# Float32 attention items whose product with v is turned and divided at the end, and three weight pieces asked for later

## The chip, the core and the metric

The kernel runs on one core of one Trainium2 chip. The metric is device microseconds for one execution, the median of three runs. A core has engines with queues of their own that run side by side: TensorE (PE) for matmuls, which writes to PSUM; VectorE (DVE) and ScalarE (ACT) for elementwise work, which read PSUM and SBUF; GpSimd (POOL), which reads SBUF alone; and SyncE (SP), whose queue issues the DMAs here. Each queue is strictly in order; engines wait for one another by semaphores.

## The reference

Windowed causal attention (4 batches, 8 heads, 576 positions, head size 64, window 128, with a bias that falls with distance), and after it two feed-forward layers over 2304 tokens, 512 to 2048 to 512. The weights are float64.

```python
scores = scale * np.matmul(q, k.transpose(0, 1, 3, 2))
scores = np.where(mask, scores + bias[None], -1000000000.0)
attn = np.exp(scores - np.max(scores, axis=-1, keepdims=True))
attn = attn / (np.sum(attn, axis=-1, keepdims=True) + 1e-09)
x = np.matmul(attn, v)            # then [tokens, 512]
h = x @ w_in
g = np.maximum(h, 0.0) + alpha * np.minimum(h, 0.0)
x = g @ w_out
# second layer: g = h * sigmoid(1.702 h), again two products
```

## The kernel before

Attention is cut into 64 items: a batch, a head, and the first 256 or the last 320 of the positions. The first 16 items (n < FP), the first 256 positions of two batches, are done in plain float32; each of their matmuls shows as two passes in the trace. All later products are done with each operand split into a high and a low part (names ending in h and l) and three matmuls, high by high, high by low and low by high.

A float32 item goes through these steps. QK (L343): scores of two chunks of 128 queries, against 128 and 256 keys, with K=64. Bias (L363, DVE): bias and mask are added and the row's least value is taken (the scores have their sign turned). Exp (L379, ACT), with the sum of each row read out by the same instruction. Reciprocal (L387 and L388, DVE) of the sum plus 1e-9. Normalization: the first chunk on DVE (L399), the second on ACT (L397). Three transpositions of 128x128 on PE (L412) and one copy out of PSUM on ACT (L419, pt). Then the product with v (L433): v stands still, pt moves, so the result x has head dimensions on partitions and queries on columns. v was copied by POOL (L329) into a tile of 128 columns that is zero but for the 64 of its head, even or odd; so the two heads of a pair add up in one PSUM tile of 128x256. After the odd head x is split (L480 on ACT, xh; L107 on DVE, xl): that is one of four blocks (c) of 128 rows of the first layer's input.

The weights come as float64, 32 pieces of 512 KB for the first layer. A piece goes: load (L131, SP), two scalings of its words on ACT (L147, L148), then on DVE sign (L152), shift (L157), add (L162), which frees its load buffer (four of them), and a split into a high part (L102 on ACT, L103 on DVE for two of them) and a low part wl (L107, DVE).

The program is written as a loop of 10 steps ahead of the first token block; each step issues parts of several items and the steps of two weight pieces. Then come token blocks of 256 with 16 steps each (f); a step is a feed-forward product h (L494, 12 matmuls, two PSUM buffers), the activation (n, L509 on ACT; g, L519 on DVE; split gh, gl) and, two steps later, the second product o (L545, 12 matmuls); one attention item is spread over two steps. The first block also takes a weight piece per step. A scheduler that runs its own timeline while it builds the program sets the order on each engine, so the order of the queues is not that of the code. The program's first feed-forward products, f=0 and 1, run in four parts, as the blocks c of x come. The later blocks, the second layer and its output are the same in both kernels.

Of the kernel before, what the change touches and what calls it, by code (L numbers as in the profile page):

```python
# [11 lines left out]
F32 = mybir.dt.float32  # L12
# [3 lines left out]
AF = mybir.ActivationFunctionType  # L16
ALU = mybir.AluOpType
PSUM = bass.MemoryType.PSUM

B, H, S, D = 4, 8, 576, 64  # L20
NT, DM, DFF = 2304, 512, 2048
P = 128
# [12 lines left out]
         chunks=((256, 128, 128, 256), (384, 128, 256, 256), (512, 64, 384, 192))),  # L35
# [12 lines left out]
FP = 2 * H  # L48
# [17 lines left out]
def tile_window_attention__then__two_mlps(  # L66
# [13 lines left out]
    nc = tc.nc  # L80
# [10 lines left out]
    ident = const.tile([P, P], F32, name="ident")  # L91
# [129 lines left out]
    def w(step, lim=2 * NF):  # L221

        names = ("load", "scale", "sign", "shift", "add", "split")
        i = wdone.get(step, 0)
        if i < min(lim, wdone.get(names[names.index(step) - 1], 0)):
            {"scale": w_scale, "sign": w_sign, "shift": w_shift, "add": w_add, "split": w_split}[step](i)
            wdone[step] = i + 1

    def w_ahead():
        if wdone.get("add", 0) >= 2 * NF and ("x", 0) not in p2:  # L230
            return
        i = wdone.get("load", 0)
        while i < min(wdone.get("add", 0) + NST, len(chunks)):
            w_load(i)
            i += 1
        wdone["load"] = i

    def w_decode(lim):
        w("sign", lim)
        w("shift", lim)  # L240
        w("add", lim)
        w_ahead()
        w("scale", lim)
# [21 lines left out]

    af = ExitStack()
    apf = af.enter_context(tc.tile_pool(name="attf", bufs=1))
    vzs = [apf.tile([P, 2, P], F32, name=f"vz{i}") for i in range(2)]
    pts = [apf.tile([P, 384], F32, name=f"pt{i}") for i in range(2)]
    relht = apf.tile([P, H, 2 * P], BF16, name="relht")  # L270

# [13 lines left out]
    st = {}  # L285
# [37 lines left out]
    @stage  # L323
    def a_split_v(n, b, u, h, U):
        nv = (2, 4)[u]
        vr = raw_of(n)[:, UCOLS[u] - nv * D : UCOLS[u]].rearrange("p (j d) -> p j d", d=D)
        if n < FP:
            d0 = (h % 2) * D
            nc.gpsimd.tensor_copy(vzs[n % 2][:, :, d0 : d0 + D], vr)  # L329
            return  # L330
        vp = ar["v", n % 2]
        nc.scalar.copy(vp[:, :nv, :D], vr)
        sub("pool", vp[:, :nv, D:], vr, vp[:, :nv, :D])
# [40 lines left out]
    @stage  # L374
    def a_exp(n, b, u, h, U):
        tt, s = tts[n % 2], sts[n % 2]
        for i, (c0, rows, kk, keys) in enumerate(U["chunks"]):
            t = tt[:rows, i * 256 : i * 256 + keys]
            nc.scalar.activation(  # L379
                t, t, AF.Exp, bias=s[:rows, i : i + 1], scale=-1.0, accum_out=s[:rows, 4 + i : 5 + i]  # L380
            )

    @stage
    def a_recip(n, b, u, h, U):
        s = sts[n % 2]
        m = len(U["chunks"])
        nc.vector.tensor_scalar(s[:, 8 : 8 + m], s[:, 4 : 4 + m], 1e-9, None, op0=ALU.add)  # L387
        nc.vector.reciprocal(s[:, 12 : 12 + m], s[:, 8 : 8 + m])  # L388

    @stage  # L390
    def a_norm(n, b, u, h, U, eng):
        tt, s = tts[n % 2], sts[n % 2]
        for i, (c0, rows, kk, keys) in enumerate(U["chunks"]):
            t = tt[:rows, i * 256 : i * 256 + keys]
            r = s[:rows, 12 + i : 13 + i]
            if eng == "act" or (eng == "mix" and i):
                nc.scalar.mul(t, t, r)  # L397
            else:
                nc.vector.tensor_scalar(t, t, r, None, op0=ALU.mult)  # L399
# [27 lines left out]
    @stage  # L427
    def a_av(n, b, u, h, U):
        if n < FP:
            x = st["x", n] = st["x", n - 1] if h % 2 else ps_a.tile([P, 512], F32, tag="a", name="x")  # L430
            pt, vz = pts[n % 2], vzs[n % 2]
            for j in range(2):
                nc.tensor.matmul(  # L433
                    x[:, j * P : 256], vz[:, j, :], pt[:, j * 256 : 256 + j * P],
                    start=(h % 2 == 0 and j == 0), stop=(h % 2 == 1 and j == 1), skip_group_check=True,
                )
            return
        vp = ar["v", n % 2]
        x = ps_a.tile([P, 512], F32, tag="a", name="x")
        js = (0, 1) if u == 0 else (2, 1, 3, 4)  # L440
        for i, j in enumerate(js):
            col, nq, oc = PTCOL[u][j]
            v = vp[:, j - U["k0"] // P, :]
            for k, p in enumerate((ar["pth"], ar["ptl"])):
                nc.tensor.matmul(  # L445
                    x[:, oc : oc + nq], v, p[:, col : col + nq],
                    start=(i == 0 and k == 0), stop=(i == len(js) - 1 and k == 1),
                    skip_group_check=True,
                )
        st["x", n] = x  # L450
# [17 lines left out]
    @stage  # L468
    def a_x3(n, b, u, h, U):
        if h % 2 == 0:  # L470
            return
        nq, c, xp = U["nq"], h // 2, xps
        if n < FP:
            xp = st["x", n]
        t = u * B * UNITS[0]["nq"] + b * nq
        done = 0
        while done < nq:
            r = (t + done) % RING
            w = min(nq - done, RING - r)
            nc.scalar.copy(xh[:, c, r : r + w], xp[:, done : done + w])  # L480
            sub("dve", xl[:, c, r : r + w], xp[:, done : done + w], xh[:, c, r : r + w])
            done += w
# [222 lines left out]


    for t in vzs:
        nc.gpsimd.memset(t, 0.0)
    for t in sts:
        nc.gpsimd.memset(t, 1.0)  # L710
    def w_first(n):
# [22 lines left out]
    for n in range(H + 2):  # L734

        a_av(n - 2)
        a_split_v(n)
        if n + 4 < H + 2:
            a_load(n + 4)
        if n >= H:  # L740
            a_load(n + 2)
        if n + 1 < H + 2:
            a_qk(n + 1)
        a_bias(n)
        w("split")
        w("sign")
        a_exp(n)
        a_recip(n - 1)
        w("shift")
        a_norm(n - 1, "mix")  # L750
        a_trans(n - 1)
        w("add")
        w_ahead()
        w("scale")
        a_x3(n - 2)
        w("split")
        w("sign")
        w("shift")
        a_pt_hi(n - 1, 0)
        a_pt_hi(n - 1, 1)  # L760
        if n + 2 < H + 2:
            a_split(n + 2)
        w("add")
        w_ahead()
        w("scale")
    n = H + 2
    a_split(n)
    for i in range(2):
# [12 lines left out]
    for s, (k, f) in enumerate(steps):  # L781
        n = H + 2 + s // 2
        norm = "mix" if k == 0 else "dve"
        if (k, f) == (KM, 0):
            pinned.append(True)
        dec = k == 0 or k == KM
        lim = min(3 * NF, max(W1, wdone["split"]) + 3) if k else W1

        def wd(*names):
            for x in names if dec else ():  # L790
                w(x, lim)

        m = n - 1
        m1_h(k, f)
        if s % 2 == 0:
            a_trans(m)
            a_qk(n)
            a_pt_hi(m, 0)
            m1_n(k, f)
            wd("sign")  # L800
            m1_g(k, f)
            a_pt_hi(m, 1)
            a_bias(n)
            wd("shift")
            a_pt_lo(m, 0)
            a_pt_lo(m, 1)
            wd("add", "scale")
            w_ahead()
            a_split(n + 1)
            a_exp(n)  # L810
            m1_lo(k, f, "dve")
        else:
            a_av(m)
            if n == FP:
                a_parts()
            a_recip(n)
            a_split_v(n)
            a_load(n + 2)
            a_norm(n, norm)
            m1_n(k, f)  # L820
            wd("sign")
            m1_g(k, f)
            a_x1(n - 1)
            wd("shift", "scale")
            a_x2(n - 1)
            wd("add")
            w_ahead()
            m1_lo(k, f, "dve")
            a_x3(n - 1)
        if k == 0:  # L830
            w("split")
        m1_o(k - (f < LAG), (f - LAG) % NF)
        if n == NI + 1 and s % 2:
            at.close()
            p2["ps"] = ctx.enter_context(tc.tile_pool(name="ps_p", bufs=1, space=PSUM))
            p2["x", 0] = ctx.enter_context(tc.tile_pool(name="p20", bufs=1))
            pre = ExitStack()
            p2["g1"] = pre.enter_context(tc.tile_pool(name="g1", bufs=3))
            p2["n1"] = pre.enter_context(tc.tile_pool(name="n1", bufs=2))
            w_ahead()  # L840
        if k == KM:
            w("split", min(3 * NF, W1 + 2 * (f - 2)))
            if f >= 8 and f % 2 == 0:
                x2_split(0, f // 2 - 4)
            if f >= 6 and f % 2 == 0 and f < 14:
                x2_load(0, f // 2 - 3)
# [117 lines left out]
```

## Time and profile before

| what | value |
|---|---|
| median of 3 runs | 968.03 us (967.75 to 969.53) |
| the profiled execution | 967.92 us, span 966.1 us |
| PE busy | 939.6 us, 97% of the span |
| DVE busy | 721.6 us, 75% |
| ACT busy | 536.4 us, 56% |
| POOL busy | 89.8 us, 9% |
| chain that ended last | PE 92%, DMA 3%, ACT 2%, DVE 1% |

The span is the time from the first to the last instruction; the run's own time is 1.8 us longer. PE is busy nearly all the time, but matmuls overlap and their ends are modelled, so the start of one and the start of the next tell more than the busy share. The rows below are from the first 140 us, where the changed code runs. Names of tiles stand without buffer numbers; L and a number are a line of the kernel.

### The profile page before, as it was taken

To read this page: it belongs to the slowest core of one execution; us is meant where nothing else is said; L and a number is where in the kernel's file an instruction comes from. 1 tells how busy PE (TensorE), PEld (TensorE's weight loads), DVE (VectorE), ACT (ScalarE), POOL (GpSimd) and SP (SyncE) were. 2 spreads that over 40 slices of the span, in tenths; PEclk is the share of its full clock that TensorE was granted. 3 is DMA by queue.
4 is the path that set the end of the run, shared out by engine and by line. 5 is a ranking of instruction groups with operands and counts; after the bars stand their busy time and mean duration, and the time that the engine had idled before them with its cause. 6 is when DMAs were issued, how large, how long until landed. Compare 5 with 4: busy or idle time off the path is not lost.

```text
span 966.1 us, 17886 instructions
## 1 busy us (share of the span) xinstructions
PE 939.6 (97%) x6536; PEld 871.2 (90%) x6536; DVE 721.6 (75%) x1789; ACT 536.4 (56%) x1343; POOL 89.8 (9%) x127
## 2 busy tenths in 40 slices
PE   5899999999999999999999999999999999999997
PEld 3579889999999999999988888888898889999997
DVE  6998967767888888887666864697233798878876
ACT  6987766666767667676534443564232644333433
POOL 1000021122222222222000000000000000000000
PEclk9999999999999999999999999999999999999999
DMA  8654521222222223212022335566432333443323
GB/s 266 187 185 148 184 79 56 78 72 66 89 67 88 67 66 89 67 66 89 1 69 81 124 112 182 186 219 200 155 113 88 140 140 114 142 142 113 132 85 109
DMA packets 43895, 112.44 MB, mean 116 GB/s; under 512 B 5024, under 2 KB 15008, under 8 KB 43808
## 3 DMA queue, kind: packets, MB, share of 16 engines
q1 hardware_dynamic: 43808, 111.31, 35.3%
q8 instruction: 51, 0.84, 0.3%
q14 instruction: 36, 0.29, 0.1%
HBM read 82.98 MB, written 28.31 MB: 115 GB/s over the span
## 4 chain that ended last, share of the span: by engine, by line
PE 92%; DMA 3%; ACT 2%; DVE 1%; issue 1%; SPq 0%; DVEq 0%; ACTq 0%
PE h L494 21%; PE h L592 20%; PE p L659 17%; PE o L545 17%; PE p L545 5%; PE x L445 3%; PE pt L412 3%; DMA ws<-in_w_out_dram 2%; PE s L352 1%; PE s L353 1%; PE s L343 1%; PE x L433 1%; ACT ws L148 1%; DMA ws<-in_w_in_dram 0%; ACT oh L102 0%
## 5 line engine op out<-in xcount | busy, mean ns | idle before, releaser
L494 PE MATMUL h<-xh,wh 128*128 128x256 f32 (+1 forms) x512 | 153.7, 302 | 1.0 <-ACT xh L480 0.7
L494 PE MATMUL h<-xh,wl 128*128 128x256 f32 (+1 forms) x512 | 153.6, 300 | 0.0
L494 PE MATMUL h<-xl,wh 128*128 128x256 f32 (+1 forms) x512 | 153.5, 300 | 0.1
L659 PE MATMUL p<-wh,oh 128*128 128x256 f32 x504 | 136.2, 284 | 1.0 <-ACT oh L102 0.6
L659 PE MATMUL p<-wl,oh 128*128 128x256 f32 x504 | 136.1, 283 | 0.0
L545 PE MATMUL o<-gh,wl 128*128 128x256 f32 x448 | 127.5, 286 | 0.0
L545 PE MATMUL o<-gh,wh 128*128 128x256 f32 x448 | 125.4, 286 | 0.0
L545 PE MATMUL o<-gl,wh 128*128 128x256 f32 x448 | 125.2, 281 | 0.0
L659 PE MATMUL p<-wh,ol 128*128 128x256 f32 x504 | 119.2, 284 | 1.0 <-DVE ol L107 1.0
L592 PE MATMUL h<-x2h,wh 128*128 128x512 f32 (+1 forms) x320 | 117.8, 368 | 0.0
L592 PE MATMUL h<-x2l,wh 128*128 128x512 f32 (+1 forms) x320 | 117.7, 368 | 0.0
L592 PE MATMUL h<-x2h,wl 128*128 128x512 f32 (+1 forms) x320 | 117.7, 368 | 0.0
L606 DVE TENSOR_TENSOR g<-h,sg 128x512 f32<-128x512 f32 (+1 forms) x80 | 51.0, 637 | 79.6 <-ACT sg L602 79.5
L602 ACT ACTIVATE sg<-h 128x512 f32<-128x512 f32 (+1 forms) x80 | 44.5, 556 | 107.2 <-PE h L592 106.9
L494 PEld LDWEIGHTS h<-xh,wh 128*128 128x128 f32 x512 | 97.9, 192 | 6.7 <-ACT xh L480 1.9
L494 PEld LDWEIGHTS h<-xl,wh 128*128 128x128 f32 x512 | 98.5, 192 | 5.0 <-DVE st L388 1.3
L494 PEld LDWEIGHTS h<-xh,wl 128*128 128x128 f32 x512 | 98.3, 192 | 2.9
L659 PEld LDWEIGHTS p<-wh,oh 128*128 128x128 f32 x504 | 96.4, 192 | 2.1 <-ACT oh L102 2.0
L659 PEld LDWEIGHTS p<-wl,oh 128*128 128x128 f32 x504 | 96.7, 192 | 0.1
L519 DVE SCALAR_TENSOR_TENSOR g<-n,beta,h 128x256 f32<-128x256 f32 x112 | 53.2, 476 | 46.6 <-ACT n L509 46.4
L659 PEld LDWEIGHTS p<-wh,ol 128*128 128x128 f32 x504 | 86.3, 192 | 1.7 <-DVE ol L107 1.6
L509 ACT ACTIVATE n<-h 128x256 f32<-128x256 f32 x112 | 42.8, 384 | 79.9 <-PE h L494 79.5
(107 smaller groups left out, 2270.7 us busy)
## 6 DMA issues: line engine op xcount, KB each, us to landing
ws<-in_w_in_dram SPq DMA_DIRECT2D x32, 512.0 KB, 3.6
ws<-in_w_out_dram SPq DMA_DIRECT2D x32, 512.0 KB, 3.9
raw<-in_u_dram SPq DMA_DIRECT2D x32, 512.0 KB, 3.4
g2d<-g SPq DMA_DIRECT2D x32, 512.0 KB, 3.4
gr<-g2d SPq DMA_DIRECT2D x32, 512.0 KB, 3.2
raw<-in_u_dram SPq DMA_DIRECT2D x16, 320.0 KB, 2.8
wd<-x2d SPq DMA_DIRECT2D x36, 128.0 KB, 3.0
out_dram<-ob SPq DMA_DIRECT2D x16, 256.0 KB, 3.9
```

The source lines that it names most:

```text
L148: pin(nc.scalar.mul(lo, lo.bitcast(U32), 2.0**-29))
L343: nc.tensor.matmul(o[:, :keys], raw[:, c0 : c0 + rows], raw[:, 256 + kk : 256 + kk + keys], start=True, stop=True)
L412: nc.tensor.transpose(banks[bank][:, dst : dst + P], src, ident)
L445: nc.tensor.matmul(x[:, oc : oc + nq], v, p[:, col : col + nq], start=(i == 0 and k == 0), stop=(i == len(js) - 1 and k == 1), skip_group_ ...
L494: nc.tensor.matmul(ph, w[:, 0, c * P : (c + 1) * P], x[:, c, r : r + n], start=(c == 0 and i == 0), stop=(c == NC - 1 and i == 2),)
L509: nc.scalar.activation(n, ph, AF.Relu, scale=-1.0)
L519: nc.vector.scalar_tensor_tensor(g, n, beta[:, f : f + 1], ph, op0=ALU.mult, op1=ALU.add)
L545: nc.tensor.matmul(o, w[:, 1, c * P : (c + 1) * P], g, start=(f == 0 and (k == KM or c % 2 == 0) and i == 0), stop=(f == NF - 1 and i == 2 ...
L592: nc.tensor.matmul(ph[:, :n], w[:, f % 2, c * P : (c + 1) * P], x[:, c, :n], start=(c == 0 and i == 0), stop=(c == NC - 1 and i == 2),)
L602: nc.scalar.activation(sg[:, :n], ph[:, :n], AF.Sigmoid, scale=1.702)
L606: nc.vector.tensor_tensor(g[:, f % 2, :n], ph[:, :n], sg[:, :n], op=ALU.mult)
L659: nc.tensor.matmul(o[:, m, :], g[:, a, m * P : (m + 1) * P], w, start=(p == 0 and m == 0 and i == 0), stop=(p == NF // 2 - 1 and i == 2), ...
```

## The change

For the 16 float32 items the weights of the softmax are no longer divided before the product with v. The exponentials are transposed as they are; pt now stands still and v moves, with a 65th column of ones, so that the product has queries on partitions and 64 columns plus the sum of the row, three matmuls of 128x65 per item (chunk 0 with its keys, chunk 1 with two blocks of keys). Two heads share one PSUM tile of 2x2x65 columns, xq. After the odd head DVE adds 1e-9 to the four sums, takes their reciprocals and multiplies the four blocks by them into a tile in SBUF, also named xq; PE transposes that back in two 128x128 steps (in a_x3) and the split into xh and xl follows as before. The sums out of the exponentials, the reciprocals per item and the normalization fall away for these items. The memsets of v's tiles write ones in place of zeros.

In the loop ahead of the token blocks every third step issues one weight piece where it issued two, so three fewer of its ten steps' twenty; four extra calls stand in the first token block.

```diff
-    vzs = [apf.tile([P, 2, P], F32, name=f"vz{i}") for i in range(2)]
+    vzs = [apf.tile([P, 2, D + 1], F32, name=f"vz{i}") for i in range(2)]
+    xq = apf.tile([P, 2, 2, D], F32, name="xq")
...
-            d0 = (h % 2) * D
-            nc.gpsimd.tensor_copy(vzs[n % 2][:, :, d0 : d0 + D], vr)
+            nc.gpsimd.tensor_copy(vzs[n % 2][:, :, :D], vr)
...
+            if n < FP:
+                nc.scalar.activation(t, t, AF.Exp, bias=s[:rows, i : i + 1], scale=-1.0)
+                continue
...
     def a_recip(n, b, u, h, U):
+        if n < FP:
+            return
...
-        for i, (c0, rows, kk, keys) in enumerate(U["chunks"]):
+        for i, (c0, rows, kk, keys) in enumerate(U["chunks"] if n >= FP else ()):
...
     def a_av(n, b, u, h, U):
         if n < FP:
-            x = st["x", n] = st["x", n - 1] if h % 2 else ps_a.tile([P, 512], F32, tag="a", name="x")
+            x = st["xq", n] = st["xq", n - 1] if h % 2 else ps_a.tile([P, 2, 2, D + 1], F32, tag="a", name="xq")
             pt, vz = pts[n % 2], vzs[n % 2]
-            for j in range(2):
+            for c, j, col in ((0, 0, 0), (1, 0, 128), (1, 1, 256)):
                 nc.tensor.matmul(
-                    x[:, j * P : 256], vz[:, j, :], pt[:, j * 256 : 256 + j * P],
-                    start=(h % 2 == 0 and j == 0), stop=(h % 2 == 1 and j == 1), skip_group_check=True,
+                    x[:, c, h % 2, :], pt[:, col : col + P], vz[:, j, :],
+                    start=(c == j == h % 2 == 0), stop=(c == j), skip_group_check=True,
                 )
+            if h % 2:
+                s = sts[n % 2]
+                r = s[:, 8:12].rearrange("p (c h) -> p c h", c=2)
+                nc.vector.tensor_scalar(r, x[:, :, :, D], 1e-9, None, op0=ALU.add)
+                nc.vector.reciprocal(s[:, 12:16], s[:, 8:12])
+                r = s[:, 12:16].rearrange("p (c h) -> p c h", c=2)
+                nc.vector.tensor_tensor(xq, x[:, :, :, :D], r.unsqueeze(3).to_broadcast([P, 2, 2, D]), op=ALU.mult)
             return
...
         if n < FP:
-            xp = st["x", n]
+            xp = ps_a.tile([P, 512], F32, tag="a", name="x")
+            for i in range(2):
+                nc.tensor.transpose(xp[:, i * P : (i + 1) * P], xq[:, i, :, :], ident)
...
-        nc.gpsimd.memset(t, 0.0)
+        nc.gpsimd.memset(t, 1.0)
...
         a_x3(n - 2)
-        w("split")
-        w("sign")
-        w("shift")
+        both = n % 3 < 2
+        if both:
+            w("split")
+            w("sign")
+            w("shift")
...
-        w("add")
-        w_ahead()
-        w("scale")
+        if both:
+            w("add")
+            w_ahead()
+            w("scale")
...
             w("split")
+            if f % 4 == 3:
+                w_decode(lim)
+                w("split")
         m1_o(k - (f < LAG), (f - LAG) % NF)
```

Two places show what the scheduler makes of it. The first is DVE's queue from the fourth low part of x (xl, the last block that f=0 and 1 need) to the first two activations g. Before:

```order
L107 TENSOR_TENSOR xl<-x,xh 128x256
L388 RECIPROCAL st_149<-st_149 128x2
L152 TENSOR_SCALAR ws<-ws 128x512
L162 ISA wd<-ws,wd 128x1024
L399 TENSOR_SCALAR tt_147<-tt_147,st_149 128x128
L157 SCALAR_TENSOR_TENSOR wd<-wd,ws 128x512
L107 TENSOR_TENSOR wl_534<-wd,wh_533 128x512
L519 SCALAR_TENSOR_TENSOR g<-n,beta,h 128x256 x2
```

And now, on the same engine at the same place (ISA is the bias or the add, by its line):

```order
L107 TENSOR_TENSOR xl<-x,xh 128x256
L157 SCALAR_TENSOR_TENSOR wd<-wd,ws 128x512
L162 ISA wd<-ws,wd 128x1024
L107 TENSOR_TENSOR wl_771<-wd,wh_770 128x512
L162 ISA wd<-ws,wd 128x1024
L363 ISA tt_146,st_148<-s,relht 128x128
L363 ISA st_148 128x1
L363 ISA tt_146,st_148<-s,relht 128x256
L363 ISA st_148 128x1
L107 TENSOR_TENSOR wl_838<-wd,wh_837 128x512
L152 TENSOR_SCALAR ws<-ws 128x512
L533 SCALAR_TENSOR_TENSOR g<-n,beta,h 128x256 x2
```

The reciprocal and the normalization are gone, and a bias and more weight steps stand ahead of g. Counted from the start of the queue to the first g, before and now: signs 18 and 23, shifts 18 and 22, adds 17 and 22, low parts wl 16 and 21, items' biases 10 and 11, xl 4 and 4; the reciprocals, additions of 1e-9 and normalizations of 10 items before, those of 4 pairs now.

The second is PE's queue at the first split item, number 16, whose scores are the products of kh and kl with q. Before:

```order
L412 MATMUL pt<-ident,tt_147 128x128
L352 MATMUL s<-kh,q 128x192
L353 MATMUL s<-kl,q 128x192
L352 MATMUL s<-kh,q 128x256
L353 MATMUL s<-kl,q 128x256
L412 MATMUL pt<-ident,tt_147 128x128 x2
L433 MATMUL x<-pt_161,vz_159 128x256
L433 MATMUL x<-pt_161,vz_159 128x128
L494 MATMUL h<-xh,wh_226 128x256
L494 MATMUL h<-xh,wh_270 128x256
L412 MATMUL pt<-ident,tt_146 128x128
L352 MATMUL s<-kh,q 128x192
```

And now:

```order
L508 MATMUL h<-xh,wl_1127 128x256
L417 MATMUL pt<-ident,tt_147 128x128
L352 MATMUL s<-kh,q 128x192
L353 MATMUL s<-kl,q 128x192
L417 MATMUL pt<-ident,tt_147 128x128 x2
L352 MATMUL s<-kh,q 128x256
L353 MATMUL s<-kl,q 128x256
L508 MATMUL h<-xh,wh_1126 128x256
L508 MATMUL h<-xl,wh_1126 128x256
L508 MATMUL h<-xh,wl_1127 128x256
L559 MATMUL o_720<-gh,wh_951 128x256
```

Before, the scores of item 17 follow those of item 16 after one item's product with v and two products h; now 51 products h and o stand between the two, with the product of item 15 and the last pair's transpositions among them.

## Rows read from the trace of the kernel before

**Rows 1.** Stretches: start and end, length, busy time by engine, clock, DMA share, GB/s.
```profile
5.38:61.96 56.58, 44.00 (x127) 29.68 (x128) 50.59 (x145) 48.08 (x118) 5.03 (x11) 1.00 0.75 227
...
80.00:100.00 20.00, 20.00 (x164) 19.39 (x163) 18.08 (x46) 15.83 (x37) 0.81 (x2) 1.00 0.53 171
120.00:140.00 20.00, 18.27 (x138) 17.33 (x136) 13.09 (x44) 14.22 (x46) 4.58 (x9) 0.91 0.26 90
125.60:129.00 3.40, 3.26 (x14) 2.86 (x15) 1.59 (x7) 1.68 (x7) 0.59 (x2) 0.50 0.59 189
```

**Rows 2.** DVE's instructions in order of time: start, length, what; ahead of the first g.
```profile
59.24 0.42 DVE L107 TENSOR_TENSOR xl<-x,xh 128x256 fp32r<-128x256 f32 x1
59.57 0.16 DVE L388 RECIPROCAL st<-st 128x2 f32<-128x2 f32 x1
59.64 0.41 DVE L152 TENSOR_SCALAR ws<-ws 128x512 int32<-128x512 int32 x1
59.96 0.69 DVE L162 CUSTOM_DVE_ANT_0 wd<-ws,wd 128x1024 uint16<-128x1024 uint16 x1
60.56 0.28 DVE L399 TENSOR_SCALAR tt<-tt,st 128x128 f32<-128x128 f32 x1
60.76 0.69 DVE L157 SCALAR_TENSOR_TENSOR wd<-wd,ws 128x512 int32<-128x512 int32 x1
61.36 0.69 DVE L107 TENSOR_TENSOR wl<-wd,wh 128x512 fp32r<-128x512 f32 x1
61.96 0.87 DVE L519 SCALAR_TENSOR_TENSOR g<-n,beta,h 128x256 f32<-128x256 f32 x2
```

**Rows 3.** Chain that ended last: start, length, engine, tile, line; two stretches.
```profile
63.44 1.36 PE h L494 x5
64.81 1.28 PE x L433 x4
...
122.74 0.41 ACT kh L102
123.14 0.32 ACT q L316
123.46 0.37 ACT pt L419
...
124.89 0.30 ACT vp L332
125.19 0.28 ACT xh L480
...
127.78 0.39 ACT n L509
128.20 0.49 DVE g L519
```

**Rows 4.** DVE in order of time: one item's bias, and what follows it.
```profile
9.19 0.29 DVE L363 CUSTOM_DVE_ANT_0 tt<-s,relht 128x128 f32<-128x128 f32 x1 [0.42 <-PE s L343]
...
9.41 0.42 DVE L363 CUSTOM_DVE_ANT_0 tt<-s,relht 128x256 f32<-128x256 f32 x1
...
9.76 0.69 DVE L162 CUSTOM_DVE_ANT_0 wd<-ws,wd 128x1024 uint16<-128x1024 uint16 x1
```

**Rows 5.** DVE's waits from 5 to 62 us: for whom, total, times, longest.
```profile
DVE ws L152 <- ACT wd L147: 2.1, 3, 1.0
...
DVE st L387 <- ACT tt L379: 1.2, 2, 0.7
```

**Rows 6.** PE in order of time: three transpositions and what follows.
```profile
76.23 0.49 PE L412 MATMUL pt<-ident,tt 128*128 128x128 f32 x3
76.65 0.37 PE L343 MATMUL s<-raw 64*128 64x128 f32 x1
```

**Rows 7.** PE in order of time: an item's product with v and what follows.
```profile
79.86 0.81 PE L433 MATMUL x<-pt,vz 128*128 128x256 f32 x4
80.43 0.36 PE L545 MATMUL o<-gh,wh 128*128 128x256 f32 x1
```

## The prediction

> **What bounds the kernel now.** I read the stretches first. TensorE (PE) is busy 44.00 of the 56.58 us from 5.38 to 61.96 and 20.00 of 20 at 80 to 100 [rows 1]: up to about 60 us it waits for others, from then on the kernel is a queue of PE work, with one hole between 120 and 140 us (18.27 of 20, granted clock 0.91) [rows 1]. So the time is the moment at which PE's unbroken stream begins, plus the PE work after it, plus the hole.
>
> Second, who sets that beginning. In that first stretch DVE is busy 50.59 of 56.58 us, ACT 48.08, PE 44.00 [rows 1]: DVE is the longest queue, idle for only 6.0 us. 61.96 is where DVE starts the first two activations g of the feed-forward stage (L519) [rows 2]. Only two buffers hold h, so PE can't start f=2 before the first g has read f=0's h. Before the change that is just not what PE waits for: g ends near 62.4, half of the pair's 0.87 us [rows 2], and PE takes up f=2 at 63.44 [rows 3], behind the scores of the next item. The slack is 1.0 us.
>
> Third, the hole. The chain of waits, all PE before it, leaves PE for ACT at 122.74 to 123.83 (kh, q, pt: 0.41 + 0.32 + 0.37 = 1.10 us), at 124.89 to 125.47 (0.30 + 0.28 = 0.58) and for n and g at 127.78 to 128.69 (0.39 + 0.49 = 0.88) [rows 3], 2.56 us of waiting. After it began the granted clock is 0.50 from 125.60 to 129.00 [rows 1], the 1.2 GHz level against 2.4 around it; of these 3.40 us 0.88 is waiting, so 2.5 us of work ran at half speed and lost about 1.25. The hole costs 3.8 us. It lies where the last float32 items meet the first split ones, and PE's queue has only two feed-forward products there between the scores of two items.
>
> **The change part by part.** First the pieces. The loop ahead of the token block asks for 17 instead of 20, but the scheduler places instructions by its own timeline, and on DVE it places more of them early, not fewer: ahead of the first g stood 16 lower parts of split weights, now 21. It fills with weights the room that the normalization left. I counted DVE's queue up to that g in both programs and price it by the step from one start to the next where DVE runs without a gap: sign 0.32 us, add 0.60, shift 0.60, lower part 0.60, reciprocal 0.07, normalization 0.20, xl 0.33 [rows 2]; a bias is 0.22 + 0.35 [rows 4].
> - more: 5 signs (1.6), 4 shifts (2.4), 5 additions (3.0), 5 lower parts (3.0), one item's bias (0.57): 10.6 us;
> - gone: for 10 items the addition of 1e-9 and the reciprocal, 0.07 each on two columns, and the normalization 0.20: 3.4 us;
> - new: for 4 pairs an addition and a reciprocal on four columns (priced as on two, 0.07 each) and a product of 128x256 out of PSUM with a broadcast factor, which no row shows; xl is the nearest, 128x256 out of PSUM with a second operand, 0.33: 1.9 us (with the normalization's 0.20 as one end and a lower part's 0.60 as the other, 1.4 to 3.0; the broadcast alone gives no reason to leave the value of xl).
>
> That is 10.6 - 3.4 + 1.9 = 9.1 us more DVE work ahead of the first g. Of it the slack takes 1.0. DVE's waits for the sums of the exponentials, 1.2 us [rows 5], go with the sums. The other waits of DVE (6.0 in all) may shrink since ACT and PE run less late against a longer DVE queue, or not; I take that they stay. The unbroken stream begins 9.1 - 1.0 - 1.2 = 6.9 us later. The bounds are 2.1 (all 6.0 us of idle time filled) and 8.1 (none).
>
> Then PE. The product with v of item 9 cost 1.28 us of the stream, at the low clock [rows 3]; it now stands ahead of the wait: -1.3. New are two transpositions per pair; for the four pairs left behind the start, at 0.42 / 3 = 0.14 us each (76.23 to 76.65) [rows 6]: +1.1. The product itself turns from passes over 256 and 128 columns (0.57 us per item at the high clock, 79.86 to 80.43 [rows 7]) into three matmuls over 65 columns, each in two passes as float32 is here. By columns that is 195 of 384, 0.29 us; if each of the six passes costs what a transposition does, 0.84. Between the ends I take the middle, 0.57, no change; over the six items left, items 10 to 15, the ends are -1.7 and +1.6.
>
> The Trainium skill, "TensorE: Matmul & The Clock Gate", section "LDWEIGHTS (loading the stationary operand)", says that loading weights takes their columns divided by 1.2 in ns, whatever is streamed. By it six loads of 128 columns are 0.64 us per item, an estimate, and the turned product would be 0.07 us dearer than before rather than cheaper, 0.4 us over six items. The transpositions' 0.14 us for a load and 128 columns doesn't contradict it, and no row shows a load bare; the sum would be 0.4 higher.
>
> ACT loses per item two reads of sums and one product, POOL copies v into a narrower tile. Both were shorter queues than DVE in that stretch (ACT 48.08, POOL 5.03 us [rows 1]), so I put them at nothing; if DVE weren't late, ACT's share would be worth what the fuller DVE queue hides. SP's loads move ahead with the additions that free their buffers; with a DMA share of 0.75 there [rows 1] that costs nothing in my sum, and should the DMA fall behind, DVE's idle time stays at the upper bound that I took.
>
> Last, the hole. In the new order the first split item's scores and the next one's are more than forty feed-forward products apart, where there were two, and all 32 weight pieces are through DVE before item 16. ACT's kh, q and pth have then time to finish under PE's stream. I take that the 3.8 us go; at the other end none does.
>
> Sum: 6.9 - 1.3 + 1.1 + 0 - 3.8 = +2.9 us. The profiled execution took 967.92 us (span 966.1, 1.8 around it), so 970.8; the median of the three runs lies 0.11 above it: 970.9.
>
> **Rivals.** (a) Not slower: the longer queue absorbs its load. In the sum DVE keeps 4.8 us of waits; if ACT and PE, now ahead of it, have all inputs ready, the start moves by 2.1 only, and 2.1 - 1.3 + 1.1 - 3.8 = -1.9; with the product at its cheap end -3.6: about 965.3. For it speaks that ACT and PE have less to do; against it that 2.1 us of the waits are for a piece's scaled words [rows 5], which the change makes no earlier. It decides where the first g starts: before about 67 us this rival holds, at 69 to 71 the forecast. (b) The later start, and the hole stays: the added dependence of xq (AV, reciprocal, product, transposition, xh) reaches PE late at the last pair. 6.9 - 1.3 + 1.1 = +6.7 alone, up to +9.6 with the start at its bound and the dear product: about 975.5. Against it speak the feed-forward products between. (c) The pieces do move: three fewer on DVE ahead of the first g, 3 x 2.12 = 6.4 us less, and faster by about as much. The order, 21 against 16 splits, speaks against it so plainly that I give it next to nothing.
>
> **How the numbers follow.** About 0.2%, 1.9 us, is what a measurement can tell here from no change. Forecast (+1.9 to +6): 0.44; (b): 0.14; together slower 0.58. Rival (a) with (c): 0.18, faster. Between them, where the start moves by some 4 us and the hole closes: 0.24. All bounds together reach from 2.1 - 1.3 + 1.1 - 1.7 - 3.8 = -3.6 (964.3) to 8.1 - 1.3 + 1.1 + 1.6 = +9.5 (977.4); the DVE product's ends add -0.5 and +1.1. Leaving about a tenth out at either end I give 965.0 to 976.5.
>
> **What the changed profile would show.** If right: the first g near 70 us (61.96 + 9.1 - 1.2), DVE busy about 59.7 us before it, PE idle just ahead of f=2 with a DVE g as releaser; then PE unbroken through the last float32 items, no half clock after the start, and no kh or vp of ACT in the chain of waits. The turned product takes 0.3 to 0.85 us per item at the high clock. I am wrong if g comes before 67 us, or if waits on xq take the place of the hole.

## The result, and the profile after

The changed kernel takes 975.49 us (median of four runs, 972.67 to 975.84) against 967.89 us (967.0 to 969.53): a ratio of 1.0070, interval 1.0047 to 1.0093. It is slower; 970.9 had been forecast, with 965.0 to 976.5 as the range. The profiled execution of the changed kernel is the quickest of its four (972.67; the others 975.25 to 975.84), so the traces account for 4.8 us (spans 970.9 and 966.1) of the 7.6 between the medians.

The stretches of the changed kernel, with the columns of [rows 1]:

```profile
5.38:71.67 66.29, 44.33 (x162) 33.94 (x162) 58.81 (x150) 51.21 (x103) 5.58 (x12) 0.93 0.77 235
60.00:64.00 4.00, 0.00 (x1) 0.03 (x1) 3.82 (x10) 3.44 (x7) 0.41 (x1) 0.85 0.72 214
64.00:68.00 4.00, 4.00 (x16) 3.02 (x16) 3.53 (x8) 2.64 (x6) 0.49 (x1) 0.50 0.75 228
80.00:100.00 20.00, 20.00 (x162) 18.94 (x161) 19.11 (x47) 17.20 (x39) 1.45 (x2) 1.00 0.60 189
100.00:120.00 20.00, 20.00 (x164) 19.01 (x163) 12.82 (x39) 9.86 (x28) 2.20 (x4) 1.00 0.32 105
120.00:140.00 20.00, 20.00 (x173) 20.00 (x172) 13.33 (x46) 13.60 (x43) 3.58 (x8) 1.00 0.28 94
62.79:76.44 13.65, 11.05 (x47) 9.91 (x48) 12.64 (x31) 10.92 (x24) 1.04 (x2) 0.50 0.62 194
```

Read against [rows 1]: the stretch up to the first g is 66.29 us long where it was 56.58, and PE has no more busy time in it (44.33, 44.00). PE does nothing from 60 to 64 us, and the granted clock is then 0.50 up to 76.44. The hole at 120 to 140 is gone: PE 20.00 of 20 at 1.00, where 18.27 at 0.91 stood. From 100 to 120 us PE is full too; in the kernel before it was not quite:

```profile
100.00:120.00 20.00, 19.31 (x145) 17.33 (x145) 18.14 (x48) 14.74 (x40) 1.80 (x3) 1.00 0.57 182
```

And DVE, busy 19.11 of 20 until 100, is down to 12.82 after that: the low part of its last weight piece starts at 106.74 us, where it started at 117.06 before.

DVE in order of time in the changed kernel, in two places: the second pair, and ahead of the first g (answers to [rows 2]). L445, L446 and L448 are the three steps on a pair's sums (add 1e-9, reciprocal, product):

```profile
37.42 0.68 DVE L162 CUSTOM_DVE_ANT_0 wd<-ws,wd 128x1024 uint16<-128x1024 uint16 x1
38.03 0.15 DVE L445 TENSOR_SCALAR st<-xq 128x4 f32<-128x4 f32 x1
38.10 0.28 DVE L363 CUSTOM_DVE_ANT_0 tt<-s,relht 128x128 f32<-128x128 f32 x1
38.30 0.68 DVE L162 CUSTOM_DVE_ANT_0 wd<-ws,wd 128x1024 uint16<-128x1024 uint16 x1
38.91 0.41 DVE L363 CUSTOM_DVE_ANT_0 tt<-s,relht 128x256 f32<-128x256 f32 x1
39.25 0.17 DVE L446 RECIPROCAL st<-st 128x4 f32<-128x4 f32 x1
39.35 0.43 DVE L152 TENSOR_SCALAR ws<-ws 128x512 int32<-128x512 int32 x1
39.85 0.69 DVE L107 TENSOR_TENSOR wl<-wd,wh 128x512 fp32r<-128x512 f32 x1
40.46 0.42 DVE L448 TENSOR_TENSOR xq<-xq,st 128x256 f32<-128x256 f32 x1
40.80 0.68 DVE L157 SCALAR_TENSOR_TENSOR wd<-wd,ws 128x512 int32<-128x512 int32 x1
...
71.23 0.52 DVE L152 TENSOR_SCALAR ws<-ws 128x512 int32<-128x512 int32 x1
71.67 0.85 DVE L533 SCALAR_TENSOR_TENSOR g<-n,beta,h 128x256 f32<-128x256 f32 x2
```

PE in order of time in the changed kernel (in brackets: idle time before it, and what ended it): the second and fourth pair's transposition back, f=2 (answers to [rows 3]), then, at the high clock, a product with v and a transposition, each with what follows (answers to [rows 6, 7]):

```profile
35.70 0.84 PE L417 MATMUL pt<-ident,tt 128*128 128x128 f32 x3
40.94 0.69 PE L488 MATMUL x<-ident,xq 128*128 128x128 f32 x2 [4.39 <-DVE xq L448]
41.42 1.38 PE L438 MATMUL xq<-vz,pt 128*128 128x65 f32 x6
...
64.00 0.66 PE L488 MATMUL x<-ident,xq 128*128 128x128 f32 x2 [4.11 <-DVE xq L448]
...
72.19 0.58 PE L508 MATMUL h<-xh,wh 128*128 128x256 f32 x1 [1.39 <-DVE g L533]
...
82.17 0.78 PE L438 MATMUL xq<-vz,pt 128*128 128x65 f32 x6
82.75 0.36 PE L508 MATMUL h<-xh,wh 128*128 128x256 f32 x1
...
97.26 0.38 PE L488 MATMUL x<-ident,xq 128*128 128x128 f32 x2
97.47 0.49 PE L417 MATMUL pt<-ident,tt 128*128 128x128 f32 x3
```

The two views belong together. The three steps on the sums take 0.07, 0.10 and 0.34 us of DVE's queue, but from the first to the end of the last it is 2.85 us (38.03 to 40.88), because whole weight steps and the next item's bias stand between them. PE's queue has the transposition of that product next, ahead of the next items' scores, and PE stands still for 4.39 us. The waits of the changed kernel from 5 to 72 us (who waits for whom, total, times, longest) say how often:

```profile
PE x L488 <- DVE xq L448: 13.8, 4, 4.4
...
DVE ws L152 <- ACT wd L147: 5.3, 6, 1.9
```

Four waits, 13.8 us, one for each pair in that stretch. The chain of waits on the page can't be used for this kernel; it breaks off near the end of the program, as its shares show (PE had 92%):

```profile
PE 1%; DVE 1%; DMA 0%; issue 0%; SPq 0%; DVEq 0%; ACT 0%; ACTq 0%
```

### The profile page after: what moved, and what is told of

The parts are those of the page before. It is cut to its first block, busy times and chain, and to the rows that moved or that the text cites. A ratio compares the mean times of both kernels' runs of the same rounds, so it can differ in the third digit from the quotient of the medians.

```text
span 970.9 us, 17890 instructions
## 1 busy us (share of the span) xinstructions
PE 936.8 (96%) x6584; PEld 874.3 (90%) x6584; DVE 718.2 (74%) x1765; ACT 528.1 (54%) x1295; POOL 89.9 (9%) x127
```

## The experiments

The numbers that the theories turned on, in one table. Pieces are the lower parts wl that stand ahead of the first g in DVE's queue; the wait is that of x for xq on PE from 5 to 72 us; PE is its busy time from 100 to 120 us; these and the first g come from one profiled execution each. Every ratio is to the kernel before as measured beside it, whose median lay between 966.55 and 967.89 us, so ratios compare better than times.

| kernel | pieces | first g | wait | PE | ratio, interval |
|---|---|---|---|---|---|
| before | 16 | 61.96 | none | 19.31 | 1 |
| changed | 21 | 71.67 | 13.8 | 20.00 | 1.0070, 1.0047 to 1.0093 |
| move_only | 16 | 61.59 | none | 18.81 | 1.0006, 0.9988 to 1.0025 |
| att_only | 21 | 73.31 | 14.1 | 20.00 | 1.0096, 1.0069 to 1.0123 |
| after_pin | 13 | 63.40 | 6.9 | 15.22 | 1.0084, 1.0059 to 1.0109 |
| before_pin | 9 | 49.61 | none | 14.03 | 1.0146, 1.0121 to 1.0171 |
| hold_0_6 | 16 | 68.91 | 8.8 | 20.00 | 1.0050, 1.0035 to 1.0065 |
| hold_0_4 | 18 | 69.03 | 7.5 | 20.00 | 1.0048, 1.0033 to 1.0063 |
| hold_3_7 | 16 | 68.17 | 9.7 | 20.00 | 1.0034, 1.0019 to 1.0048 |
| two_steps | 19 | 68.21 | 9.9 | 20.00 | 1.0048, 1.0027 to 1.0068 |
| late_turn | 16 | 63.80 | 1.9 | 20.00 | 1.0016, 1.0001 to 1.0032 |
| late_two_steps | 15 | 64.30 | 0.2 | 19.69 | 1.0013, 1.0001 to 1.0026 |
| no_norm | 14 | 56.02 | none | 16.47 | 0.9917, 0.9887 to 0.9947 |
| before_hold_4_5 | 13 | 58.30 | none | 16.40 | 1.0026, 1.0006 to 1.0046 |

**The two halves of the change, each alone.** move_only is the kernel before with the loop of the changed one (`both = n % 3 < 2` and the four extra calls), att_only the changed kernel with `both = True` and without those calls.

> The kernel before, with only the three weight pieces asked for later (the loop's every third step issues one piece, four extra calls in the first token block). Theory 1 (what counts is DVE's queue as the scheduler lays it): the queue is that of before, 48.7 us of steps and 16 low parts ahead of the first g, so 968 us within 2, first g at about 62 us. Rival (the pieces are what the code says): three pieces of 2.1 us less ahead of g, first g near 56 us and about 962 us, or a later block starved and slower by several us.

> The changed kernel without the move of the three weight pieces. Theory 1: DVE's queue is the changed kernel's, 57.9 us of steps and 21 low parts ahead of the first g, so first g near 71.7 us and 972 to 976 us, as with the move. Rival (the move is part of the cost or softens it): more than 3 us away from the changed kernel's 975.5, on the side of slower by some 6 us if the move relieves DVE.

Measured: 966.89 us (964.42 to 969.55) and 975.87 (973.93 to 976.56). Both came as theory 1 had them: the move by itself does nothing that can be told. But for a few neighbouring steps and loads that change places, the scheduler puts the pieces into the same places of the queues whichever step of the code asks for them, so the loss is the turned product's. The two traces also show what one trace is worth: with nearly the same order on DVE, the first g came at 71.67 us in the changed kernel and at 73.31 in att_only, so a difference of under 2 us between two first g says little.

**All weight steps of the loop held in the order of the code**, in both kernels:

```diff
+    pinned.append(True)
     for n in range(H + 2):
...
+    pinned.clear()
```

> The changed kernel with the weight steps of the loop ahead of the token blocks held behind what the code issues before them on their engine, so that attention's instructions pass them. 13 low parts and 40.4 us of DVE steps stand ahead of the first g where 21 and 57.9 stood. Theory 1 (the pieces ahead of g make it late): first g at 5.4 + 40.4 x 1.05 + 6 of waits, about 54 us and not later than 60, PE's stream begins 12 us or more earlier than in the changed kernel, and the time falls to 958 to 967 us (some comes back because the last pieces now are late in the first block). Theory 2 (the chain of xq: product with v, reciprocal, multiplication, transposition back): the chain is still there, first g not before 68 us, 972 to 976 us.

> The kernel before with the same hold on the weight steps: 9 low parts and 31.5 us of DVE steps ahead of the first g (before 16 and 48.7). Theory 1: the first g moves to about 50 us, where PE's own work at the low clock or the loads bound it, but 23 pieces are left for the first block, where DVE's queue up to the 15th g is 108 us of steps against 93, so the block starves PE: 962 to 978 us, with PE waiting for weights between 60 and 120 us. Theory 2 says nothing of this kernel, which has no xq; by it nothing but the block's starvation changes, so slower than before.

Measured: 974.52 (973.53 to 974.86) and 980.52 (979.72 to 980.95). The gain expected of after_pin missed, and its first g (63.40) is later than the 60 us it was to have at most; theory 2's first g of 68 or later missed as well, though its range of time holds. before_pin started as expected (49.61) and starved as expected, and its time is 2.5 us above its range of 962 to 978. The first g does come earlier, 8.3 and 12.4 us, and then PE starves. The stretch from 100 to 120 us of the changed kernel held:

```profile
100.00:120.00 20.00, 15.22 (x113) 13.35 (x112) 18.99 (x48) 15.91 (x36) 3.11 (x5) 1.00 0.57 177
```

and of the kernel before held:

```profile
100.00:120.00 20.00, 14.03 (x91) 12.48 (x91) 19.09 (x48) 16.39 (x41) 3.10 (x4) 0.91 0.50 166
```

PE's longest wait in that stretch of after_pin is for the low part of a piece:

```profile
103.19 0.39 PE L508 MATMUL h<-xh,wl 128*128 128x256 f32 x1 [1.49 <-DVE wl L107]
```

PE is down to 15.22 and 14.03 of 20 with DVE at 19: pieces that don't stand ahead of the first g have to be prepared behind it, while the stream already asks for them, and what DVE does for the activations and items stands in the same queue. An early start is worth something only with enough pieces ready. That made a new theory, a balance: hold fewer steps, so that 16 pieces are ahead as in the kernel before.

**Held in part.** The same two lines, at n = 0 to 5 (hold_0_6) and 0 to 3 (hold_0_4) in att_only, and at n = 3 to 6 (hold_3_7) in the changed kernel.

> The changed kernel without the move, its weight steps held in the order of the code in the first six steps of the attention loop only; 16 pieces then stand ahead of the first g on DVE (21 in the changed kernel, 16 in the kernel before, 13 in the fully held one). Theory of balance (the first g waits for DVE's queue, but DVE must also have prepared pieces enough for the 130 us after it): first g at 63 to 68 us, PE's stream from there, PE at least 19.8 of 20 us busy at 120 to 140, 962 to 969 us. Rival, the chain through xq costs the time whatever the queue holds: first g at 70 or later, 973 to 977 us. Rival, any hold starves the stream of pieces: PE under 18 of 20 us at 100 to 120, 973 us or more.

> The same with the hold in the first four steps only; 18 pieces stand ahead of the first g. Balance: between the two, first g at 66 to 70 us, no starved stretch after it, 966 to 972 us, and above the run with 16 pieces. Rival of the chain: 973 to 977 us. Rival of starving: less than in the run held for six steps, so a lower time than that one.

> The changed kernel with the move, held only in steps 3 to 6 of the attention loop; 16 pieces ahead of the first g again, but the early pairs run in the order of the changed kernel. Balance: the count of pieces decides, so first g at 63 to 69 us and 962 to 970 us, within 3 us of the run held in the first six steps. Chain through xq, which is longest in the early pairs (the second pair's x was 4.4 us late on xq): 971 us or more, since those pairs are not held.

Measured: 972.19 (971.34 to 973.58), 972.21 (970.82 to 973.61), 970.33 (968.96 to 973.02). The balance fails as the whole story: all three times lie above its ranges (by 3.2, 0.2 and 0.3 us), and with the 16 pieces of the kernel before, and no starved stretch at 100 to 120, the first g still comes at 68 to 69 us, not at 62. Nor is the chain's 973 to 977 (971 or more for hold_3_7) right. The stretch up to the first g and two of PE's waits in hold_0_6 say what is left. The stretch:

```profile
5.38:68.91 63.53, 44.34 (x162) 34.49 (x162) 49.70 (x130) 44.53 (x88) 4.91 (x12) 1.00 0.70 203
```

and PE's transpositions of the third and fourth pair in the same kernel:

```profile
50.58 0.66 PE L488 MATMUL x<-ident,xq 128*128 128x128 f32 x2 [3.23 <-DVE xq L448]
61.80 0.66 PE L488 MATMUL x<-ident,xq 128*128 128x128 f32 x2 [3.88 <-DVE xq L448]
```

DVE is busy 49.70 us, less than the 50.59 of [rows 1], and idle for 13.83, where 6.0 stood. It is still the busiest engine, but its work no longer accounts for the start: PE stands at the transpositions back, and what DVE needs of PE stands behind them. DVE's wait for PE in the same kernel (from 5 to 72 us), its bias into a tile that PE has yet to transpose:

```profile
DVE tt L363 <- PE pt L417: 5.3, 4, 3.5
```

**The wait itself.** late_turn asks for the transposition back and the split one loop step later; two_steps leaves out the 1e-9 and takes the reciprocal of the column of sums itself, so that two DVE steps stand where three stood; late_two_steps does both.

```diff
-        a_x3(n - 2)
+        a_x3(n - 3)
...
     n = H + 2
+    a_x3(n - 3)
```

```diff
-                r = s[:, 8:12].rearrange("p (c h) -> p c h", c=2)
-                nc.vector.tensor_scalar(r, x[:, :, :, D], 1e-9, None, op0=ALU.add)
-                nc.vector.reciprocal(s[:, 12:16], s[:, 8:12])
                 r = s[:, 12:16].rearrange("p (c h) -> p c h", c=2)
+                nc.vector.reciprocal(r, x[:, :, :, D])
```

> The changed kernel with one line moved: a pair's x is transposed back (and split into xh, xl) one loop step later, so that PE has the next item's scores and transposition to do while DVE divides. Nothing is held. 16 pieces and 47.2 us of DVE steps stand ahead of the first g (21 and 57.9 in the changed kernel; 16 and 48.7 in the kernel before). Theory of the wait in PE's queue: what cost the time is that PE stands behind the transposition until DVE's three steps on the sums are through (13.8 us in four waits), DVE's longer queue is only what was filled in behind it. Then the waits of x on xq fall under 5 us, the first g comes at 61 to 66 us and the time is 963 to 969 us. Rival, DVE's load: the same three steps and all pieces remain, so first g at 67 us or later and 970 to 974 us, as in the held kernels with 16 pieces.

> The changed kernel with DVE's chain on the sums cut from three steps to two: the reciprocal is taken of the column of sums itself, without the step that adds 1e-9. 19 pieces and 53.7 us of DVE steps ahead of the first g. Theory of the wait in PE's queue: the chain loses one of its three places in DVE's queue, so the waits of x on xq fall by about a third (13.8 to about 9 us), first g at 67 to 70 us, 970 to 974 us. Rival, only the load on DVE counts: four steps of 0.15 us go, so within 1 us of the changed kernel, 974 to 976 us.

> Both edits: the transposition one loop step later and the chain in two steps. 15 pieces and 44.8 us of DVE steps ahead of the first g. Theory of the wait in PE's queue: waits of x on xq under 3 us, first g at 58 to 64 us; DVE's steps up to the 15th g are 92.0 us (before 92.9), so the stream should not starve, and the time is 960 to 967 us, at or below the kernel before. Rival, DVE's load: 969 to 973 us.

Measured: 968.24 (964.98 to 970.49), 970.88 (969.11 to 972.54), 967.58 (965.74 to 969.12). The first two came as the theory of the wait in PE's queue had them, first g included; the third is 0.58 us above its range, and its first g (64.30) just behind it: with the wait gone, a shorter DVE queue brings nothing more that can be told. PE in late_turn around the second pair and at f=2:

```profile
39.42 0.90 PE L417 MATMUL pt<-ident,tt 128*128 128x128 f32 x3
40.12 0.63 PE L488 MATMUL x<-ident,xq 128*128 128x128 f32 x2
40.98 1.51 PE L438 MATMUL xq<-vz,pt 128*128 128x65 f32 x6 [0.23 <-ACT pt L424]
...
64.32 0.58 PE L508 MATMUL h<-xh,wh 128*128 128x256 f32 x1 [1.29 <-DVE g L533]
```

and late_turn's stretches up to the first g and at the place of the old hole:

```profile
5.38:63.80 58.42, 45.68 (x162) 34.89 (x162) 48.58 (x130) 42.36 (x88) 5.28 (x12) 1.00 0.70 219
120.00:140.00 20.00, 20.00 (x171) 19.87 (x171) 14.79 (x47) 14.79 (x48) 4.38 (x10) 1.00 0.30 93
```

The transposition at 40.12 has no idle time before it, where the changed kernel had 4.39 us. The same three steps on the sums, the same pieces and the same products are in the program, and by the ratios some 5 of the 7 us are back, with the hole still closed. Nothing was held here: with the transposition later the scheduler by itself puts 16 pieces ahead of the first g, not 21. So late_turn takes away the wait and the five pieces together; no run takes the wait away and keeps the 21.

None of these beats the kernel before. late_turn's profiled span is shorter (963.2 against 966.1), but that execution is among its quickest, and twelve runs put its median 0.16% above.

**The division left out, and a hold in the kernel before.** no_norm is the kernel before without the reciprocals and products of the float32 items (the weights aren't divided by their sums, so it computes something else); before_hold_4_5 has it whole, held at n = 4 and 5 by the two lines above.

> The kernel before with the division by the sums left out for the float32 items (neither reciprocal nor the two products on the 128x128 and 128x256 tiles); nothing else is turned. DVE has 41.4 us of steps and 14 pieces ahead of the first g, against 48.7 us and 16 pieces. If DVE's load in the attention stage by itself sets the time, the first g comes at 54 to 58 us and the time falls to 958 to 963 us. If what counts is also how many pieces are ready (its steps up to the 15th g are 93.2 us against 92.9), the earlier start is lost in a stream that waits for pieces at 90 to 130 us, and the time is 965 to 971 us.

> The kernel before, with its weight steps held in the order of the code in the fifth and sixth step of the attention loop; nothing of the turned product is in it. 13 pieces and 41.7 us of DVE steps stand ahead of the first g (16 and 48.7 without the hold; 14 and 41.4 in the kernel without the division), and 94.0 us up to the 15th g (92.9; 93.2). The run without the division came out at 960.99 us; two theories of why. If it gained by when DVE's queue lets the first g through, this kernel, with nearly the same counts and the division in it, gains as much: first g at 54 to 58 us, 960 to 965 us, and it beats both kernels. If it gained by the division's shorter chain from the exp sums to the transposition of the weights, this kernel gains nothing: first g at 58 us or later, 966 to 972 us.

Measured: 960.99 (954.6 to 964.03) and 969.79 (966.69 to 972.12). So with the whole division gone, 6.5 us are to be had, as the theory of DVE's load had it. The two have nearly the same counts in DVE's queue and not the same time, so the counts don't explain that gain, and before_hold_4_5 came as the theory of the division's chain had it (58.30, no gain). Both starve at 100 to 120 us (PE 16.47 and 16.40 of 20), no_norm in spite of its gain. Whether the gain is the division's chain or its time on DVE these runs don't settle, for the first g is 2.3 us apart as well.

## Why the prediction was right, and where not

**The number: inside the range, in part by luck.** The time is 4.6 us above the forecast and 1.0 under the end of the range. Of the 4.6, the traces put 1.9 on the start, with 0.3 less behind it, as told below; most of the rest, 2.8 us, lies between executions of the same kernel and is no term of the sum.

**The start later: right in kind, too small.** f=2 starts at 72.19 us, 8.75 after [rows 3] (8.82 by PE's own row, 63.37); 6.9 had been forecast. By terms: DVE's work ahead of the first g rose by 58.81 - 50.59 = 8.2 us (9.1 forecast); its idle time went from 6.0 to 7.5, up 1.5 where -1.2 had been forecast; the slack between g and f=2 gave 1.0 (1.48 to 0.52), as forecast. 8.2 + 1.5 - 1.0 = 8.7. The failed term is the idle time. The waits for the exp sums did go, but those for scaled words grew from 2.1 [rows 5] to 5.3 us, and the new chain through xq was left out of this step, with the 13.8 us that PE stands at it.

**Why 21 pieces: the prediction's reason was wrong.** "It fills with weights the room that the normalization left" doesn't hold. late_turn has the same room and 16 pieces. What late_turn takes away is PE standing at the transposition, so that is what opens the room; that the scheduler then has little else than pieces to give DVE is argued, not shown. The count was read rightly from the order, so the price (9.1 for 8.2) came out nearly right with the wrong cause, which is luck. Two comparisons put rough sizes on it: with 16 pieces instead of 21, the first g comes 3.5 us earlier in hold_3_7 (68.17 against 71.67) and 4.4 in hold_0_6 (68.91 against 73.31 in att_only), though the wait shrank there too, to 9.7 and 8.8 us; with most of it gone and 16 pieces still, late_turn's comes another 4.4 to 5.1 earlier (63.80).

**Behind the start: right in size.** The turned product takes 0.58 us per item (82.17 to 82.75, and the same at the other five items), 0.57 forecast as the middle of 0.29 and 0.84. No row had spoken for the middle, so that it fits is luck. The transposition back takes 0.21 us a pair (97.26 to 97.47), 0.28 forecast, so four pairs cost 0.8, not 1.1. DVE's product on xq moves its queue on by 0.34 us (40.46 to 40.80), 0.33 forecast. By the rule of the Trainium skill weighed in the prediction ("TensorE: Matmul & The Clock Gate", section "LDWEIGHTS (loading the stationary operand)") the product's six loads would have taken 0.64 us, an estimate; the measured 0.58 for the whole product lies below that. The half clock lasts until 76.44, 4.25 us into the stream; in the kernel before, PE's pace from one start to the next changes from 0.21 to 0.12 us at 67.59, 4.2 us after its f=2, so the clock adds nothing there:

```profile
63.37 0.58 PE L494 MATMUL h<-xh,wh 128*128 128x256 f32 x1
...
67.38 0.38 PE L494 MATMUL h<-xh,wh 128*128 128x256 f32 x1
67.59 0.28 PE L494 MATMUL h<-xl,wh 128*128 128x256 f32 x1
67.71 0.28 PE L494 MATMUL h<-xh,wl 128*128 128x256 f32 x1
```

Item 9's product now lies at 69.42, ahead of the first g, as forecast.

**The hole: right.** PE is busy 20.00 of 20 at 120 to 140 us at a clock of 1.00. Its price of 3.8 us is not measured by itself: 2.56 us of it were counted from the chain, while PE's idle time there was 20 - 18.27 = 1.73; but the 0.69 us that PE was idle at 100 to 120 are gone too, which no term counted. With the forecast's own -1.3 and -3.8 the sum is 8.75 - 1.3 + 0.8 + 0 - 3.8 = 4.45 us. The last product h of the first layer starts 4.23 us later than before (568.91 in the kernel before, 573.14 in the changed one), so the sum holds within 0.2; the spans differ by 4.8.

```profile
568.91 0.40 PE L494 MATMUL h<-xh,wl 128*128 128x512 f32 x1
573.14 0.40 PE L508 MATMUL h<-xh,wl 128*128 128x512 f32 x1
```

What the other 2.8 us between the medians are, no row shows. One candidate is a start that varies, as between the changed kernel and att_only; no trace shows the slower executions.

**The rivals.** (a), the absorbed load, falls by its own mark: first g at 71.67, not before 67. (b) named 975.5, which is close to the median, but its mechanism is wrong: the hole is gone (its upper end, +9.6, is +9.5 by its own terms; nothing hangs on that). What it looked for, PE late on xq, is there, only at the first four pairs and not the last, and inside the step that the forecast had sized by DVE's queue alone. (c), the pieces really moving, is settled by move_only: they don't. The expected sign in the profile, a DVE g as releaser of f=2, is there; that it ends only 1.39 us of PE's idle time, and xq the 4.11 us of the last wait before it, is what the prediction didn't see.

## What to carry to other kernels

An engine with an in-order queue should not get an instruction at its head that needs several steps of another, fully loaded engine: 0.5 us of new work on DVE left PE standing for up to 4.4 us at a time, and asking for the consumer one step later gave most of it back. Where a scheduler orders the queues, read the order for what stands directly behind a new chain, on each engine that the chain crosses, not only for counts. An earlier start is worth what the resource behind it can feed: the two kernels held throughout started 8 and 12 us sooner, and one gained nothing that can be told, the other lost 1.5%.

## What the hardware showed unexpectedly

The granted clock reads full in the first stretches, though PE's pace there is that of the low level. Passes of 128x256 in late_turn, in a stretch whose clock is given as 1.00:

```profile
65.13 0.41 PE L508 MATMUL h<-xh,wh 128*128 128x256 f32 x1
65.34 0.41 PE L508 MATMUL h<-xl,wh 128*128 128x256 f32 x1
```

with the stretch:

```profile
64.00:68.00 4.00, 3.68 (x17) 3.68 (x18) 3.85 (x11) 4.00 (x10) 0.00 (x0) 1.00 0.44 163
```

and in the changed kernel, where the clock is given as 0.50 and then as 1.00:

```profile
72.99 0.41 PE L508 MATMUL h<-xh,wh 128*128 128x256 f32 x1
73.21 0.41 PE L508 MATMUL h<-xl,wh 128*128 128x256 f32 x1
...
79.92 0.28 PE L559 MATMUL o<-gh,wl 128*128 128x256 f32 x1
80.04 0.28 PE L559 MATMUL o<-gh,wh 128*128 128x256 f32 x1
```

Steps of 0.21 us belong to the low level and 0.12 to the high one; late_turn's 0.21 under a clock of 1.00 is the low level. So in the early stretches of these traces the pace from one start to the next tells the clock, not the column, and the 1.00 of the first stretches above is not to be read as full speed.
